# One idle product after the products with the inverse, in a chunked recurrence on one Trainium2 core

## The chip, the cores and the metric

The program runs on one core of one Trainium2 chip. The metric is the device time of one execution in microseconds (us); of several runs the median is taken. Engine names in the profile: PE is TensorE's products, PEld its weight loads, DVE is VectorE, ACT is ScalarE, POOL is GpSimd and SP is SyncE, which issues most DMAs. PEclk is the share of TensorE's clock that was granted: 0.50 is 1.2 GHz and 1.00 is 2.4 GHz.

## The reference

Three stages follow one another. The first is a recurrence over 768 time steps for 32 heads with a state of 40 by 40:

```python
for t in range(S):
    y[:, :, t] = einsum('bhd,bhde->bhe', r_t, state)
    Sa = einsum('bhde,bhe->bhd', state, a_t)
    state = state * w_t[:, :, None, :] - einsum('bhd,bhe->bhde', Sa, b_t) + einsum('bhd,bhe->bhde', v_t, k_t)
```

Its result is the input of a mixture of eight experts (top 2 of 8, 3072 tokens, width 320, inner width 1024), and that of a dense layer with inner width 2048 and a leaky rectifier, whose result is the output. Inputs and output are float32.

## The kernel before, in words

The recurrence is done in 12 chunks of 64 time steps. Inside a chunk the dependence of later steps on earlier ones is a triangular system. The kernel prepares, ahead of a chunk, decay factors by scans on VectorE (wq, lines 76 to 99), float16 stacks and their transposes by DMA (stack, tr, lines 101 to 107), score products (ks, lines 121 to 134), and the inverse of small diagonal blocks, which POOL builds row by row (t_step, line 148) and VectorE transposes into TT (t_fin, line 151).

The heads are handled in four groups of four pairs. Each group g has a PSUM bank of its own, bk[g] (128 partitions by 512 float32 columns). For each group a chunk takes four steps (two halves blk, two quarters h of 16 rows each). A step is:

- c_x (lines 163 to 174): products with the state (L170, recorded at the helper's line 167) and with what the chunk already has (also L167), into partitions 64 to 79 and 96 to 111 of bk[g]; ScalarE copies them to x (L174).
- c_u (lines 175 to 181): eight products of x with the inverse TT, 32 rows by 32 columns of the array each, in two bands (f = 0 and 1) into partitions 0 to 31 and 32 to 63 of the same bank (L179). A float32 product leaves two records in the trace, so one call of c_u leaves 16. Then ScalarE copies the two bands to VU (L181), which the next step of this group reads.

After the four steps c_s (lines 182 to 194) updates the group's state: products at L188, then VectorE (L190, L193) and POOL (L194). The output of the chunk (y_u, y_s, y_y, lines 196 to 222) follows, with products at L206, L214 and L219, and the router's logits of the next stage (L341 to L348).

The order of the work: run (line 226 on) gives each piece a key and traces the pieces in the order of the keys, so that the four groups are shifted against each other and the preparation runs about three chunks ahead. The TileContext (line 860) is built with schedule_with_timeline_sim=True: a planner then orders the instructions of every engine from their dependences. On the chip each engine runs its instructions in that fixed order. The constant s.idf (line 48) is the 128 by 128 float32 identity used for transposes.

The second stage has its products at L550 and L564, the third at L660 and L670; the change does not touch them.

Of the kernel before, what the change touches and what calls it, by code (L numbers as in the profile page):

```python
# [8 lines left out]
F16 = mybir.dt.float16  # L9
# [20 lines left out]
class Attn:  # L30
# [132 lines left out]
    def c_x(s,c,g,blk,h):  # L163
        nc=s.nc; K=s.K[c]; aT=s.aT[c%s.cfg['NA']]; VU=s.VU[c%2]; p0=64*(c%2); cs=slice(32*blk+16*h,32*blk+16*h+16); st=[True]*2
        px=s.bk[g]
        def mm(f,c0,n,l,r):
            q=64+32*f; nc.tensor.matmul(px[q:q+16,c0:c0+n],l,r,start=st[f],stop=True,skip_group_check=True); st[f]=False  # L167
        if c:
            for j in range(2):
                for f in range(2): i=4*g+2*j+f; mm(f,80*j,80,aT[:,i,cs],s.S[:,i,0:80])  # L170
        for z in range(4):
            for f in range(2): mm(f,40*z,40,K['g',f][:,4*g+z,cs],VU[:,f,4*g+z,:])
        x=s.x[g]
        nc.scalar.activation(x[p0:p0+48],px[64:112,0:160].rearrange("p (z d)->p z d",d=40),AF.Copy,scale=-0.125)  # L174
    def c_u(s,c,g,blk,h):
        nc=s.nc; TT=s.K[c]['TT']; VU=s.VU[c%2]; p0=64*(c%2); x=s.x[g]; n=32
        pu=s.bk[g][:,0:160].rearrange("p (a d)->p a d",a=4)
        for z in range(4):
            for f in range(2): nc.tensor.matmul(pu[32*f:32*f+n,z],TT[p0+32*f:p0+32*f+32,16*h:16*h+n,2*(4*g+z)+blk],x[p0+32*f:p0+32*f+32,z],start=h==0 and z==0,stop=True,skip_group_check=True)  # L179
        for f in range(2):  # L180
            q=64-64*f+32*blk; nc.scalar.activation(VU[q:q+n,f,4*g:4*g+4],pu[32*f:32*f+n],AF.Copy)  # L181
    def c_s(s,c,g):
# [681 lines left out]
```

## Time and profile before

| what | value |
|---|---|
| median of 3 runs | 1518.03 us (1511.66 to 1520.21) |
| profiled execution, its own time | 1532.47 us |
| its span (first to last instruction) | 1530.7 us |
| mean granted TensorE clock over the span | 0.87 |
| TensorE busy | 1215.9 us (79%) |
| VectorE busy | 892.4 us (58%) |
| ScalarE busy | 583.8 us (38%) |
| POOL busy | 481.8 us (31%) |

The profile is of one execution. Busy time is the union of the records of an engine; the ends of products are modelled, so a busy TensorE is not one at its peak. The chain of waits is followed back from the last instruction, at each step to what released it; its shares add up over the span or over the stretch that was asked for. Idle time of an engine that is not on that chain costs nothing by itself.

### The profile page before, as it was taken

How to read it: one execution, taken by the hardware profiler on the slowest of the kernel's cores; microseconds unless marked ns; L12 is line 12 of the kernel's file. 1: busy time of each engine (PE TensorE's matmuls, PEld its weight loads, DVE VectorE, ACT ScalarE, POOL GpSimd, SP SyncE). 2: the span in 40 equal slices, each digit the busy share in tenths (PEclk: the TensorE clock that was granted, in tenths of full speed). 3: DMA queues.
4: the chain of work that ended last, by engine and by line, in shares of the span. 5: the costliest groups of instructions: out<-in, count | busy, mean ns of one | idle time of the engine just before them, and what ended most of it. 6: DMA issues, size and time to landing. Idle time of an engine off the chain costs nothing.

```text
span 1530.7 us, 37727 instructions
## 1 busy us (share of the span) xinstructions
PE 1215.9 (79%) x15975; PEld 915.0 (60%) x15975; DVE 892.4 (58%) x2029; ACT 583.8 (38%) x1343; POOL 481.8 (31%) x559
## 2 busy tenths in 40 slices
PE   1358788878877879724879779779896799999998
PEld 0247677767766768624647557557575565555555
DVE  6897665664666487664654555679732764443221
ACT  1345345444545543431333223234321444334422
POOL 7464415224153252125222022030002526423422
PEclk9999776676888876757999889899998899999999
DMA  8679887768867755459745767375312522110000
GB/s 224 136 142 171 154 153 134 147 123 156 158 132 133 136 105 125 87 186 164 165 136 165 211 186 202 115 204 151 111 56 67 119 65 52 35 35 18 18 18 20
DMA packets 305937, 188.15 MB, mean 123 GB/s; under 512 B 260894, under 2 KB 276355, under 8 KB 304891
## 3 DMA queue, kind: packets, MB, share of 16 engines
q1 hardware_dynamic: 293103, 156.91, 46.6%
q0 software_dynamic: 10368, 16.84, 4.5%
q10 hardware_dynamic: 2288, 11.90, 2.4%
q8 instruction: 127, 2.08, 0.6%
q14 instruction: 51, 0.42, 0.1%
HBM read 105.24 MB, written 23.18 MB: 84 GB/s over the span
## 4 chain that ended last, share of the span: by engine, by line
PE 47%; DVE 20%; DMA 19%; POOL 5%; issue 4%; ACT 2%; SPq 2%; another core or an unknown queue 1%; ACTq 0%; DVEq 0%; POOLq 0%
PE ph L660 10%; PE po L670 10%; PE po L564 9%; PE ph L550 6%; DMA wf<-w 6%; PE bk L167 5%; DMA kbt<-stk 4%; PE bk L179 2%; DVE l L519 2%; DVE kb L99 2%; DMA w<-wi 2%; DMA N<-nd 1%; DVE Dt L82 1%; DVE S L193 1%; DMA nd<-ns 1%
## 5 line engine op out<-in xcount | busy, mean ns | idle before, releaser
L550 PE MATMUL ph<-xT,h 128*128 128x372 f16 (+2 forms) x680 | 151.2, 353 | 81.0 <-DVE gl L553 54.2
L552 ACT ACTIVATE gh<-ph 128x372 f16<-128x372 f32 (+2 forms) x136 | 68.1, 510 | 258.4 <-PE ph L550 245.9
L528 POOL DMA_INDIRECT xr<-xs,ix x56 | 81.4, 1453 | 254.9 <-DMA xT<-xr 234.2
L550 PEld LDWEIGHTS <-h 128*128 128x128 f16 x680 | 68.8, 102 | 126.5 <-issue 90.0
L664 POOL TENSOR_TENSOR gl<-hc,gh 128x512 f16<-128x512 f32 x80 | 91.9, 1157 | 146.7 <-ACT gh L663 146.5
L167 PE MATMUL bk<-S,aT 128*16 128x80 f32 x1408 | 113.5, 286 | 30.7 <-DVE S L193 20.9
L167 PE MATMUL bk<-VU,g 128*16 128x40 f32 x3072 | 135.1, 237 | 2.7 <-ACT VU L181 1.8
L181 ACT ACTIVATE VU<-bk 32x160 f32<-32x160 f32 x384 | 112.4, 293 | 62.3 <-PE bk L179 51.0
L564 PE MATMUL po<-h,gh 128*124 128x320 f16 x448 | 135.3, 304 | 1.0 <-ACT gh L552 0.6
L564 PE MATMUL po<-h,gl 128*124 128x320 f16 x448 | 134.5, 305 | 0.1
L564 PE MATMUL po<-l,gh 128*124 128x320 f16 x448 | 134.4, 303 | 0.0
L660 PE MATMUL ph<-xT,wih 128*128 128x512 f16 (+2 forms) x560 | 125.2, 354 | 7.8 <-DVE hc L662 4.5
L564 PEld LDWEIGHTS <-gh 128*124 128x124 f16 x896 | 122.7, 137 | 10.7 <-ACT gh L552 1.1
L662 DVE SCALAR_TENSOR_TENSOR hc<-ph,hc 128x512 f32<-128x512 f32 (+2 forms) x112 | 68.3, 612 | 98.2 <-ACT hc L661 97.2
L179 PE MATMUL bk<-x,TT 32*32 32x40 f32 x3072 | 122.8, 240 | 0.0
L670 PE MATMUL po<-woh,gh 128*128 128x320 f16 x384 | 114.1, 301 | 4.5 <-ACT gh L663 4.0
L167 PEld LDWEIGHTS bk<-VU,g 128*16 128x16 f32 x3072 | 111.1, 121 | 10.2 <-issue 4.2
L670 PE MATMUL po<-wol,gh 128*128 128x320 f16 x384 | 113.8, 301 | 0.0
L638 POOL DMA_INDIRECT yy<-yd,slot x48 | 48.7, 1014 | 204.0 <-DMA yd<-y 157.2
L179 PEld LDWEIGHTS bk<-x,TT 32*32 32x32 f32 x3072 | 103.4, 149 | 13.4 <-issue 3.8
L670 PE MATMUL po<-woh,gl 128*128 128x320 f16 x384 | 109.4, 301 | 0.0
L663 ACT ACTIVATE gh<-hc 128x512 f16<-128x512 f32 (+2 forms) x112 | 62.5, 566 | 119.2 <-PE po L670 66.4
(286 smaller groups left out, 2471.4 us busy)
## 6 DMA issues: line engine op xcount, KB each, us to landing
wf<-w SPq DMA_DIRECT2D x24, 512.0 KB
w<-wi SPq DMA_DIRECT2D x16, 768.0 KB
wf<-w SPq DMA_DIRECT2D x32, 320.0 KB
w<-wo SPq DMA_DIRECT2D x16, 640.0 KB
kb<-kb SPq DMA_DIRECT2D x24, 320.0 KB
yd<-y ACTq DMA_DIRECT2D x7, 1085.0 KB
w<-wz SPq DMA_DIRECT2D x24, 208.8 KB
aa<-aa SPq DMA_DIRECT2D x12, 320.0 KB
```

Of the source, the lines that this page charges most:

```text
L167: q=64+32*f; nc.tensor.matmul(px[q:q+16,c0:c0+n],l,r,start=st[f],stop=True,skip_group_check=True); st[f]=False
L179: for f in range(2): nc.tensor.matmul(pu[32*f:32*f+n,z],TT[p0+32*f:p0+32*f+32,16*h:16*h+n,2*(4*g+z)+blk],x[p0+32*f:p0+32*f+32,z],start=h== ...
L181: q=64-64*f+32*blk; nc.scalar.activation(VU[q:q+n,f,4*g:4*g+4],pu[32*f:32*f+n],AF.Copy)
L528: c=e*NJ+j; nc.gpsimd.indirect_dma_start(out=xr[0:PT,j],out_offset=None,in_=s.xs,in_offset=bass.IndirectOffsetOnAxis(ap=s.ix[0:PT,c:c+1],a ...
L550: for n,(t,k,i) in enumerate(ps): nc.tensor.matmul(ph[:,0:N],w(t,k,f),xT[:,j0:j1,i,0:PT],start=n==0,stop=n==7)
L552: nc.scalar.activation(o,ph[:,0:N],AF.Relu)
L564: nc.tensor.matmul(po[0:PT,0:DM],a[:,f,c],b[:,DM*f:DM*f+DM],start=n==0,stop=n==23); n+=1
L660: for n,(t,k,i) in enumerate(ps): nc.tensor.matmul(ph[:,0:N],w(t,k,f),xT[:,b0:b1,i,:],start=n==0,stop=n==7)
L662: nc.vector.scalar_tensor_tensor(c,ph[:,0:N],0.01,c,ALU.mult,ALU.max)
L663: nc.scalar.activation(gh[:,f,0:N],c,AF.Copy)
L664: (nc.vector if g<2 else nc.gpsimd).tensor_tensor(gl[:,f,0:N],c,gh[:,f,0:N],ALU.subtract)
L670: nc.tensor.matmul(po[:,0:DM],a[:,f,128*(b-b0):128*(b-b0)+128],bb[:,f,:],start=n==0,stop=n==47); n+=1
```

## The change

A new helper, warm, issues one matmul: the stationary operand is 64 columns, the moving operand 256 columns read twice (512 in all), both taken from the identity read as float16. It writes partitions 64 to 127 of the group's whole bank and starts a new accumulation there. Nobody reads the result: the next c_x or c_s of the group overwrites it. c_u calls it once, after its products and before the two copies to VU.

```diff
+    def warm(s,t):
+        w=s.idf.bitcast(F16); m=bass.AP(tensor=w.tensor,offset=w.offset,ap=[w.ap[0],[0,2],[1,256]])
+        s.nc.tensor.matmul(t[64:128,0:512],w[:,0:64],m,start=True,stop=True,skip_group_check=True)
     def c_u(s,c,g,blk,h):
         nc=s.nc; TT=s.K[c]['TT']; VU=s.VU[c%2]; p0=64*(c%2); x=s.x[g]; n=32
         pu=s.bk[g][:,0:160].rearrange("p (a d)->p a d",a=4)
         for z in range(4):
             for f in range(2): nc.tensor.matmul(pu[32*f:32*f+n,z],TT[p0+32*f:p0+32*f+32,16*h:16*h+n,2*(4*g+z)+blk],x[p0+32*f:p0+32*f+32,z],start=h==0 and z==0,stop=True,skip_group_check=True)
+        s.warm(s.bk[g])
         for f in range(2):
             q=64-64*f+32*blk; nc.scalar.activation(VU[q:q+n,f,4*g:4*g+4],pu[32*f:32*f+n],AF.Copy)
```

## Rows read from the trace of the kernel before

**Rows 1.** The page: busy tenths and granted clock in 40 equal slices.
```profile
PE   1358788878877879724879779779896799999998
...
PEclk9999776676888876757999889899998899999999
```

**Rows 2.** Busy time by stretch; columns as in the first line, one stretch a row.
```profile
core 0: us, PE busy (x) PEld busy (x) DVE busy (x) ACT busy (x) POOL busy (x), PEclk, DMA share, GB/s
...
97.00:650.00 553.00, 451.44 (x11083) 393.30 (x11083) 369.56 (x912) 269.40 (x766) 199.10 (x309) 0.77 0.72 137
```

**Rows 3.** The chain that ended last, whole program: by engine, and by line.
```profile
PE 47%; DVE 20%; DMA 19%; POOL 5%; issue 4%; ACT 2%; SPq 2%; another core or an unknown queue 1%; ACTq 0%; DVEq 0%; POOLq 0%
...
by line: PE ph L660 9.7%; PE po L670 9.5%; PE po L564 8.8%; PE ph L550 6.3%; DMA wf<-w 5.6%; PE bk L167 4.8%; issue 4.2%; DMA kbt<-stk 4.1%; PE bk L179 2.1%; DVE l L519 1.8%; DVE kb L99 1.6%; DMA w<-wi 1.5%; DMA N<-nd 1.4%; DVE Dt L82 1.4%;
```

**Rows 4.** The chain from 97 to 650 us, by line.
```profile
by line: PE bk L167 13.1%; DMA kbt<-stk 10.6%; issue 6.3%; PE bk L179 5.9%; DVE S L193 3.7%; DMA nd<-ns 3.3%; DMA N<-nd 3.3%; DVE kb L99 3.1%; DVE Dt L82 2.5%; DMA ut<-us 2.4%; DMA kb<-kb 2.4%; DVE stk L106 2.1%; POOL T L148 1.9%; DMA kb<-x
```

**Rows 5.** The page's groups: busy us, mean ns of one, idle before them.
```profile
L179 PE MATMUL bk<-x,TT 32*32 32x40 f32 x3072 | 122.8, 240 | 0.0
```

**Rows 6.** Waits, 97 to 650 us: us in total, times, longest.
```profile
ACT x L174 <- PE bk L167: 123.5, 116, 6.5
...
ACT VU L181 <- PE bk L179: 51.0, 61, 5.3
```

**Rows 7.** The chain in order of time, 261 to 296 us: start, length, what.
```profile
254.37 6.87 DMA kbt<-stk
261.29 0.48 PE sc L129 x8
...
265.54 0.67 PE bk L179 x14
...
275.30 0.68 PE bk L179 x16
...
282.18 0.52 PE pt L95 x4
282.72 0.48 DVE kb L99
```

**Rows 8.** Busy time by stretch inside that period; columns as in rows 2.
```profile
258.00:261.00 3.00, 1.59 (x65) 1.28 (x60) 0.33 (x2) 0.60 (x2) 2.53 (x7) 0.99 0.73 134
...
264.00:266.00 2.00, 2.00 (x51) 1.58 (x49) 1.68 (x5) 1.19 (x5) 0.31 (x2) 0.50 1.05 75
...
278.00:280.00 2.00, 2.00 (x30) 1.50 (x27) 0.00 (x0) 0.93 (x4) 0.00 (x0) 0.50 0.22 82
...
282.00:285.00 3.00, 3.00 (x111) 2.68 (x108) 2.40 (x6) 1.69 (x4) 1.49 (x2) 1.00 0.12 29
```

**Rows 9.** The chain in order of time, third stage, clock 1.00.
```profile
1265.08 1.73 PE ph L660 x8
```

**Rows 10.** TensorE in order of time, second stage, clock 0.50: start, length, instruction.
```profile
909.18 2.23 PE L550 MATMUL ph<-xT,h 128*128 128x496 f16 x5 [8.25 <-DVE gl L553]
911.20 1.45 PE L550 MATMUL ph<-xT,l 128*128 128x496 f16 x3
```

**Rows 11.** TensorE in order of time, recurrence, clock 0.50.
```profile
275.23 0.75 PE L179 MATMUL bk<-x,TT 32*32 32x40 f32 x16
275.90 0.71 PE L167 MATMUL bk<-S,aT 128*16 128x80 f32 x6
276.55 1.28 PE L179 MATMUL bk<-x,TT 32*32 32x40 f32 x32
277.76 0.31 PE L167 MATMUL bk<-S,aT 128*16 128x80 f32 x1
```

**Rows 12.** What TensorE's products waited for, 97 to 650 us.
```profile
PE bk L167 <- DVE S L193: 20.9, 9, 4.4
PE sc L129 <- DMA kbt<-stk: 20.4, 11, 3.6
...
PE bk L167 <- ACT VU L181: 11.4, 11, 2.7
```

## The prediction

> **What bounds the kernel now.** I read the page's slices first, to find the stage in which the changed function runs. TensorE is at seven tenths or more from the fourth slice on, and its granted clock is full at the start and for most of the second half; in slices 5 to 17 between them it reads six to eight tenths [rows 1]. The table by stretch makes this exact: the recurrence runs from 97 to 650 us, TensorE (PE) is busy 451.44 of 553 us, the mean granted clock is 0.77, and the 16 DMA engines are 72% busy [rows 2]. As the clock has two levels, 1.2 GHz (0.50) and 2.4 GHz (1.00), a mean of 0.77 is about half of the time at each.
>
> Next the chain of waits. Over the whole program PE holds 47% of it, but most of that lies behind the recurrence [rows 3]. Cut to the recurrence, the chain is mixed: the products that make x (L167) 13.1%, the products with the inverse (L179) 5.9%, and besides them DMA transposes, VectorE lines and the block inverse on POOL [rows 4]. So TensorE ends the stage for part of the time only, and no engine for all of it. The groups give the sizes: L179, the line behind which the change puts its product, is 122.8 us of busy time in 3072 records, and PE sat idle 0.0 us before it [rows 5]. Twice a step it is ScalarE that waits for TensorE: the x copy 123.5 us for L167, the VU copy 51.0 us for L179 [rows 6].
>
> Last I went through one period. The chain runs from the DMA transpose that ends at 261.24 through 30 pieces of PE alone, 21 us, to 282.70, and then goes over to VectorE [rows 7]. In the middle of these 21 us, in each of the eight stretches from 264 to 280, PE is busy 2.00 of 2.00 us and the clock is 0.50 all the same; from 282 to 285 it is 1.00 [rows 8]. Of the pieces in it, L179 has a gap of ten us, from the 14 records at 265.54 to the 16 at 275.30 [rows 7].
>
> **The change, part by part.** Nothing is removed. Each of the 192 calls of c_u (12 chunks, 4 groups, 4 steps; 3072 records are 192 times 16) gets one weight load and one product. No DMA is added or moved, and no queue of SP or POOL is passed. The product reads a constant and writes partitions 64 to 127 of the group's bank. The x copy has read them before c_u can begin, since c_u reads x, so the product adds no wait of its own; the VU copies read partitions 0 to 63. What it does is to stand in TensorE's queue: behind it are the next products of another group, mostly c_x, c_u or c_s, and behind those ScalarE and VectorE.
>
> *Length.* The trace has such a product in another stage. A 128x512 f16 product takes 1.73/8 = 0.216 us at clock 1.00 [rows 9]. At 0.50, five products of 496 columns take 911.20-909.18 = 2.02 us, 0.404 each, so 0.42 us for 512 columns [rows 10]. The bounds are 0.22 and 0.42.
>
> *Change of shape.* The inverse products use 32 rows by 32 columns of the array; the x products use 128 rows. One c_u of 16 records is followed by an x product after 275.90-275.23 = 0.67 us, two of 32 records after 277.76-276.55 = 1.21 us; so 16 records cost 0.54 us, and 0.13 us is left for the change of shape [rows 11]. The idle product (128 by 64) fits neither neighbour, so I count one more such change for each, 0.13 us; the lower bound is nothing, the upper 0.26 where the next one is again a c_u. Total per product: 0.35 us at 1.00, 0.55 us at 0.50. The Trainium skill, TensorEngine Tiling (Array Packing), section Key Properties, says that a change of tiling mode, unlike a change of tile, drains TensorE; by that rule every idle product pays it going in or out, and it speaks against the change. The 0.13 us of the row agrees. Without any drain the sum below would be about 7 us lower.
>
> *How many are on the path.* L179 has 2.1% of the whole chain, 0.021 x 1530.7 = 32 us, out of 122.8 us busy: 26%, or 50 of 192 calls [rows 3, 5]. These cost 50 x 0.35 = 17.5 to 50 x 0.55 = 27.5 us. The 21 us of PE alone lie at 0.50, so I take a value towards the upper end: 24 us.
>
> *The other 142* are in stretches where something else is late: 142 x 0.35 to 0.55 is 50 to 78 us of new TensorE work, covered by the 553-451 = 102 us in which PE is idle now [rows 2]. What hides it is PE's waits for the state update (20.9 us), the transposed kbt (20.4 us) and the VU copy (11.4 us) [rows 12]. Where such a cover is shorter than the products ahead of it, the remainder shows. Bounds: none, or all that exceeds the cover; with some 64 us against 102 us spread unevenly I take 10 us.
>
> *What the clock gives back.* If the products lift the clock, the chain's PE work shrinks. The two lines have 4.8% + 2.1% of the chain, 105 us [rows 3]; were all of it at 0.50 now and at 1.00 after, 52 us would be saved. The other bound is nothing. I take 9 us, near nothing, for three reasons in the rows. First, PE was busy without a break from 264 to 280 us and stayed at 1.2 GHz [rows 8], so a fuller TensorE alone doesn't raise it; the product there puts off other products and fills no pause. Second, it stands behind c_u and not in the waits: the clock read 0.99 from 258 to 261 us, when PE was busy 1.59 of 3 us, and was 0.50 afterwards [rows 8], and a product of 0.2 us issued ahead of a wait leaves most of that wait empty. Third, there are ten us without c_u in that very stretch [rows 7]. The Trainium skill, TensorE: Matmul & The Clock Gate, section Why this matters for your kernels, advises to keep TensorE busy to have the full clock; by that advice the saving would be near the 52 us. Rows 8 disagree for this kind of product.
>
> **Sum:** 24 + 10 - 9 = +25 us. Against the profiled execution, 1532.47 us (span 1530.70 and 1.77 around it), that gives 1557. The profiled execution lies 14.4 us above the median of the three runs, 1518.03; with the same difference the median becomes **1543 us**.
>
> **Rivals.**
> *A, the clock rises (faster).* The idle product is 512 columns of 128 rows where c_u fills 32 rows, and it comes 192 times, so it could hold TensorE at 2.4 GHz through most of the stage. For: about half of the stage is at 0.50, and the chain's longest PE stretch with it [rows 2, 7, 8]. Against: the three reasons above. Time: of the 52 us that L167 and L179 can save, 40; the products at full clock cost 50 x 0.35 = 17.5 us: 1518 - 22 = 1496. It decides if the granted clock from 97 to 650 us goes above about 0.9.
>
> *B, no change.* The planner, which orders the instructions from the program's dependences, puts the products where PE would wait anyway, or what they cost and what the clock gives back are equal: 1518. This is also the case of a change that does nothing. For: PE idles 102 us of the stage [rows 2]. Against: it is idle 0.0 us before L179 [rows 5], and the product follows at once.
>
> *C, the step's own loop becomes longer.* If the VU copies are held until the idle product is over (the bank guarded as a whole), each exposed step waits 0.35 to 0.55 us more. ScalarE waited for L179 in 61 places already [rows 6]; nothing in the regions (0 to 63 against 64 to 127) requires it. With half of the 192 steps exposed, 96 x 0.45 = 43 us on top: 1518 + 25 + 43 = 1586.
>
> **How the numbers follow.** Forecast 0.55, A 0.22, B 0.15, C 0.08. About 0.5% (7.6 us) is what a measurement of this kernel can tell from no change; faster is A (0.22), same is B (0.15), slower is the forecast with C (0.63). The forecast's own range comes from its bounds, 17.5 + 0 - 9 to 27.5 + 20 - 0: 1527 to 1565. The stated range reaches to B and to the weaker half of A on one side, 1503, and towards C on the other, 1572; some 0.1 is left out at each end.
>
> **What would show it.** In the new profile: 192 products of 512 columns, of 0.22 to 0.42 us each; the recurrence about 25 us longer, TensorE's busy time in it up by 50 us or more, its granted clock between 0.75 and 0.85, the stages behind it unchanged; in the period shown, still long PE stretches at 0.50. I am wrong about the clock if the mean is above 0.9; about the cover if PE's idle time stays near 100 us while the stage gets longer; about C's cause if the VU copies begin only after the idle product's end.

## The result, and the profile after

The changed kernel takes 1526.07 us (median of 20 runs, 1513.46 to 1542.87) where the kernel before takes 1518.11 (20 runs, 1505.41 to 1524.99). The ratio of the mean times is 1.0061, 95% interval 1.0035 to 1.0088: slower by 0.0061 x 1518 = 9 us, with 5 to 13 inside the interval. Two of the 20 runs of the change, 1540.33 and 1542.87 us, were in a slower state and are left out of the ratio. The sign was forecast, the size was not: 25 us were forecast.

The two traced executions would tell the opposite (span 1520.3 us after, 1530.7 before), since the one of before lies 14 us above its median and the one after 4 us below. So I read the recurrence by itself. First the time at which the first and the last VU copy start, in the kernel before, in a second trace of it, in the change and in a second trace of the change (line numbers have moved by four):

```profile
L181 ACT ACTIVATE VU<-bk x384: 291/294/296, 100.6 to 649.0; 32x160 f32<-32x160 f32 x192
```

```profile
L181 ACT ACTIVATE VU<-bk x384: 291/294/296, 102.1 to 644.3; 32x160 f32<-32x160 f32 x192
```

```profile
L185 ACT ACTIVATE VU<-bk x384: 292/294/297, 103.3 to 650.7; 32x160 f32<-32x160 f32 x192
```

```profile
L185 ACT ACTIVATE VU<-bk x384: 291/294/298, 103.2 to 651.2; 32x160 f32<-32x160 f32 x192
```

The last copy starts at 649.0 and 644.3 us before, at 650.7 and 651.2 after. The page's slices and the table by stretch of the change answer to [rows 1, 2]:

```profile
PE   1358899988998999934879779797896899999998
...
PEclk9998788888889997856999999899998899999999
```

```profile
97.00:650.00 553.00, 500.97 (x11242) 399.67 (x11242) 366.17 (x916) 267.94 (x764) 201.92 (x311) 0.85 0.71 137
```

TensorE's busy time has gone up by 501 - 451 = 50 us, as forecast, and the granted clock from 0.77 to 0.85. In this window of 553 us TensorE is idle 52 us where it was 102. The chain of the same stretch shows what this means, against [rows 4]; the second line is that of the second trace of the change:

```profile
by line: PE bk L167 13.8%; PE bk L182 10.4%; DMA kbt<-stk 9.5%; PE bk L177 6.0%; issue 4.8%; DMA N<-nd 3.1%; DMA nd<-ns 2.9%; DMA ut<-us 2.3%; DVE kb L99 2.3%; POOL tmp L148 2.2%; POOL T L148 2.1%; PE bk L192 2.1%; DVE S L197 2.0%; PE yy L2
```

```profile
by line: PE bk L167 11.7%; DMA kbt<-stk 9.7%; PE bk L182 8.6%; issue 5.3%; PE bk L177 4.7%; DMA N<-nd 3.8%; DMA ut<-us 3.3%; POOL tmp L148 3.2%; POOL T L148 2.9%; DMA nd<-ns 2.5%; DMA kb<-kb 2.0%; DVE S L197 1.7%; DVE kb L99 1.7%; DMA kb<-x
```

L177 is the idle product: 6.0% of 553, 33 us of the chain, and 4.7%, 26 us, in the second trace. Counted along the chain from 97 to 650 us, 85 of the 192 idle products stand in it, and 69 in the second trace. The products with the inverse (L182 now) have risen from 5.9% to 10.4% and 8.6%: more of the stage waits for TensorE than before. One period in order of time, the counterpart of [rows 7]:

```profile
254.49 6.32 DMA kbt<-stk
260.85 0.61 PE sc L129 x8
...
262.60 0.56 PE bk L177
263.17 0.69 PE yy L223 x32
...
274.44 0.33 PE bk L177
274.77 0.53 PE bk L167 x16
...
279.32 0.52 PE pt L95 x4
```

The stretch of PE alone begins at 260.85 instead of 261.29 and ends at 279.84 instead of 282.70, though six idle products stand in it; each takes 0.56 us of the chain at 1.2 GHz and 0.33 at 2.4. Its clock, against [rows 8]:

```profile
268.00:270.00 2.00, 2.00 (x23) 1.31 (x24) 1.23 (x3) 0.59 (x2) 0.36 (x2) 0.50 1.03 208
270.00:272.00 2.00, 2.00 (x56) 1.74 (x52) 1.94 (x4) 0.30 (x1) 0.00 (x0) 0.72 1.25 183
272.00:274.00 2.00, 2.00 (x54) 1.91 (x54) 1.89 (x11) 0.41 (x2) 0.62 (x1) 1.00 1.31 90
```

It rises at about 271 us, after three idle products; before, it read 0.50 in every stretch up to 280. One period shows what happened in it and no more; that the clock follows the product is read from the mean over the recurrence. Last, the waits of ScalarE, against [rows 6], and two places in order of time:

```profile
ACT x L174 <- PE bk L167: 88.0, 112, 4.0
ACT VU L185 <- PE bk L177: 85.2, 118, 3.3
```

```profile
267.35 0.47 PE L182 MATMUL bk<-x,TT 32*32 32x40 f32 x6
...
267.75 0.95 PE L95 MATMUL pt<-idf,Dt 104*128 104x104 f32 x4
...
268.64 0.64 PE L177 MATMUL bk<-idf 128*64 128x512 f16 x1
...
269.31 0.60 ACT L185 ACTIVATE VU<-bk 32x160 f32<-32x160 f32 x2 [1.94 <-PE bk L177]
```

The VU copies wait for the idle product (L177) and not for the products whose result they read: here those are done before 268, the planner has put transposes between them and the product, and the copies start at the product's end. In both traces of the change none of the 192 pairs starts before its product's end, although the copies read partitions 0 to 63 and the product writes 64 to 127. So the program guards them against each other whatever the partitions; whether it goes by the whole bank or by the columns, which overlap in every version, no run separates. The wait of the VU copies rose from 51.0 to 85.2 us. That of the x copies fell from 123.5 to 88.0, so that the two together stay where they were, 174.5 and 173.2 us.

### The profile page after: what moved, and what is told of

The parts are those of the page before. It is cut to its first block, busy times and chain, and to the rows that moved or that the text cites. A ratio compares the mean times of both kernels' runs of the same rounds, so it can differ in the third digit from the quotient of the medians.

```text
span 1520.3 us, 38111 instructions
## 1 busy us (share of the span) xinstructions
PE 1260.7 (83%) x16167; PEld 917.8 (60%) x16167; DVE 887.5 (58%) x2029; ACT 583.3 (38%) x1343; POOL 484.9 (32%) x559
## 4 chain that ended last, share of the span: by engine, by line
PE 50%; DMA 20%; DVE 18%; POOL 4%; issue 3%; ACT 2%; SPq 2%; ACTq 0%; DVEq 0%; POOLq 0%
PE ph L664 9%; PE po L674 9%; PE po L568 8%; DMA wf<-w 7%; PE ph L554 6%; PE bk L167 5%; PE bk L182 4%; DMA kbt<-stk 4%; PE bk L177 2%; DVE l L523 2%; DMA N<-nd 2%; DVE wam L513 1%; DVE kb L99 1%; DVE Et L88 1%; DMA nd<-ns 1%
## 5 line engine op out<-in xcount | busy, mean ns | idle before, releaser
L182 PE MATMUL bk<-x,TT 32*32 32x40 f32 x3072 | 149.3, 234 | 4.1 <-issue 2.3
L182 PEld LDWEIGHTS bk<-x,TT 32*32 32x32 f32 x3072 | 115.5, 145 | 43.7 <-issue 20.7
L167 PE MATMUL bk<-VU,g 128*16 128x40 f32 x3072 | 114.3, 223 | 0.0
L167 PE MATMUL bk<-S,aT 128*16 128x80 f32 x1408 | 99.8, 266 | 9.8 <-ACT VU L185 4.7
L513 DVE TENSOR_REDUCE wam<-wf 128x1 f32<-128x1024 f32 (+1 forms) x35 | 46.3, 1325 | 98.2 <-DMA wf<-w 97.9
```

## The experiments

Every ratio is to the kernel before on the same chip, in five rounds; chips differ by some 10 us (before: 1516 to 1526), so ratios are compared. The granted clock is that of 97 to 650 us. In the traces of the change, e2 and e3 all other instructions come in one and the same order; e1, e5, e6 and e11 share a second one; each other run with an idle product has its own.

**Once more before, once more after.**

> The kernel before, once more, for a second trace of it and to see what two equal programs differ by. Every theory: 0.997 to 1.003, the granted clock in the recurrence 0.76 to 0.79. Theory 'order' (a part of what the products do is that the planner puts the other instructions in another order) wants the recurrence to end near 650 us here, against 635 us with the 32 by 32 product of 16 columns; if it ends near 640 us, most of that difference was chance in one trace.

> The changed kernel on the same chip as the others: 1.003 to 1.009 of before, clock 0.84 to 0.86 in the recurrence. If chips differ in what the clock gives back, it can lie outside, between 0.998 and 1.012.

Measured: 1.0002 (0.9971 to 1.0034) and 1.0076 (1.0040 to 1.0113). The stretch from 97 to 650 us, of before and of the change:

```profile
97.00:650.00 553.00, 455.04 (x11110) 396.08 (x11112) 376.53 (x923) 270.03 (x767) 204.17 (x312) 0.76 0.71 137
```

```profile
97.00:650.00 553.00, 500.82 (x11241) 401.55 (x11241) 365.62 (x916) 266.98 (x764) 202.21 (x310) 0.85 0.71 137
```

The clocks and TensorE's busy times repeat. The last VU copy of the second trace of before, 644.3 us, lies between the 650 and the 640 that the expectation named. The change costs 9 to 12 us.

**Length and clock, at the change's own order.** e3 keeps the product and cuts it to 16 columns; e2 keeps its 512 columns and fills 32 of the 128 rows.

```diff
-        w=s.idf.bitcast(F16); m=bass.AP(tensor=w.tensor,offset=w.offset,ap=[w.ap[0],[0,2],[1,256]])
-        s.nc.tensor.matmul(t[64:128,0:512],w[:,0:64],m,start=True,stop=True,skip_group_check=True)
+# e3
+        w=s.idf.bitcast(F16); m=bass.AP(tensor=w.tensor,offset=w.offset,ap=[w.ap[0],[1,16]])
+        s.nc.tensor.matmul(t[64:128,0:16],w[:,0:64],m,start=True,stop=True,skip_group_check=True)
+# e2
+        w=s.idf.bitcast(F16)[0:32]; m=bass.AP(tensor=w.tensor,offset=w.offset,ap=[w.ap[0],[0,2],[1,256]])
+        s.nc.tensor.matmul(t[64:128,0:512],w[:,0:64],m,start=True,stop=True,skip_group_check=True)
```

> The idle product keeps its shape (128 by 64), place and count and has 16 columns in place of 512. What is left is the change of shape and the wait of the VU copies behind it. 'Clock gives back': clock 0.76 to 0.78, time 1.004 to 1.010 of before, for 50 products on the path at some 0.13 to 0.3 us. 'Covered': 0.998 to 1.003.

> As the run with 32 by 32, but 32 rows by 64 columns, a shape that none of its neighbours has. 'Clock gives back': clock 0.76 to 0.81, time 1.015 to 1.03 of before; above the 32 by 32 run by the price of the change of shape, some 5 us. 'Covered': 1.003 to 1.009, as the change.

Measured: e3 1.0037 (1.0011 to 1.0062), e2 1.0168 (1.0142 to 1.0194). Of e2 the stretch and the chain of the stretch:

```profile
97.00:650.00 553.00, 516.00 (x10809) 406.49 (x10810) 351.94 (x854) 258.94 (x738) 200.53 (x312) 0.76 0.68 134
```

```profile
by line: PE bk L167 21.4%; PE bk L182 15.2%; PE bk L177 9.4%; DMA kbt<-stk 7.0%; issue 4.2%; PE bk L192 3.5%; PE sc L129 2.8%; PE ys L210 2.7%; PE yy L223 2.6%; DMA ut<-us 2.2%; DVE kb L99 2.0%; PE yy L351 1.6%; PE pt L91 1.4%; DMA kb<-kb 1
```

and of e3 the stretch; then the VU copies of e2 and of e3:

```profile
97.00:650.00 553.00, 494.39 (x11160) 429.10 (x11159) 362.12 (x899) 266.77 (x761) 201.84 (x309) 0.76 0.71 135
```

```profile
L185 ACT ACTIVATE VU<-bk x384: 291/294/298, 103.8 to 675.7; 32x160 f32<-32x160 f32 x192
```

```profile
L185 ACT ACTIVATE VU<-bk x384: 291/294/297, 102.8 to 659.3; 32x160 f32<-32x160 f32 x192
```

Three runs with one order now stand in a row: a product of hardly any length costs 0.37%, 6 us; the full length at the same clock of 0.76 costs 1.68% x 1526 = 26 us, so length is 20 us; and the product of 128 rows, which has the same length and a clock of 0.85, costs 9 us (12 on the other chip), so the clock gives back 14 to 16 us. By their intervals each of these differences can be off by 6 or 7 us; e2 and e3 ran on one chip, the change on two others. The last VU copy gives the same order: 659.3 us in e3, 675.7 in e2, 650.7 and 651.2 in the change, so 16 us for the length and 25 back.

That e2's array shape is another than the change's could be a rival to the clock. The chain speaks against it: at the same clock one idle product takes as long in e2 as in the change, 0.56 and 0.33 us.

```profile
262.54 0.56 PE bk L177
...
269.29 0.33 PE bk L177
```

For e2 this is "clock gives back" and not "covered", which wanted 1.003 to 1.009; e3, 1.0037, lies between the two theories. Above the 32 by 32 run by some 5 us, as expected too, e2 is not: it is 40 us above it. And a share of the chain is no price: 118 idle products with 52 us (9.4% of 553) stand in e2's chain, and the kernel is 26 us slower.

**The held copies.** e4 issues the product behind the two copies instead of ahead of them.

```diff
-        s.warm(s.bk[g])
         for f in range(2):
             q=64-64*f+32*blk; nc.scalar.activation(VU[q:q+n,f,4*g:4*g+4],pu[32*f:32*f+n],AF.Copy)
+        s.warm(s.bk[g])
```

> The idle product is issued behind the two VU copies, not ahead of them, so that the copies no longer wait for it and it waits for them. If the held copies are a good part of the cost (rival C), the clock stays at 0.83 to 0.87 and the time falls to 0.992 to 1.001 of before. If they cost nothing, it is 1.003 to 1.009 as the change. If TensorE's own wait for the copies is worse, over 1.012.

Measured: 1.0077 (1.0048 to 1.0105), with the clock at 0.85 again.

```profile
97.00:650.00 553.00, 490.82 (x11136) 384.63 (x11138) 363.40 (x898) 266.77 (x758) 201.29 (x309) 0.85 0.71 135
```

Without held copies it is no faster. There the product waits for the copies in place of the other way round, and the order is another, so this doesn't prove that holding them is free; it shows that nothing is won by turning the wait about.

```profile
PE bk L177 <- ACT VU L184: 11.4, 10, 2.5
```

**More of it, and another order for the same shape.** e8 calls warm twice in a row; e15 uses 48 stationary columns, w[:,0:48] into t[64:112], in place of 64.

> The change's product twice in each call, 384 products in all. The second has the shape of the first, so it adds length and work for the clock but no change of shape. If length is cheap and the clock pays for it: clock 0.88 or more in the recurrence, 1.000 to 1.008 of before. If length costs what 34 us for 192 products suggest less what the clock still gives: 1.012 to 1.030.

> The change's product, 128 rows and 512 columns, with 48 stationary columns in place of 64: the array shape (128 by 64) and the work over time are nearly the same, but the planner puts the other instructions in another order. 'Order' moves it by up to 10 thousandths: 0.997 to 1.015, clock 0.83 to 0.87. If order plays no part for this shape: 1.005 to 1.009, as the change.

Measured: e8 1.0247 (1.0209 to 1.0285) at a clock of 0.90; e15 1.0049 (1.0015 to 1.0083) at 0.85. The stretch of e8:

```profile
97.00:650.00 553.00, 501.32 (x10804) 368.16 (x10805) 350.87 (x823) 255.20 (x725) 196.86 (x305) 0.90 0.67 131
```

With a second product the clock goes from 0.85 to 0.90 and the time up by 1.7 to 1.9%, some 27 us: the clock doesn't pay for it, though e8's own order is in this too. e15, the change's shape in another order, comes out as the change does within the noise.

**Shape.** e1, e5, e6 and e11 use 32 stationary columns into t[64:96] and share one order. e1 has 32 rows and 512 columns, e5 32 rows and 16 columns (the shape of the products with the inverse), e6 128 rows and 512 columns, e11 128 rows and 16 columns (the shape of the products for x).

```diff
+# e5 (e1: 512 columns; e6: all rows of s.idf, 512 columns; e11: all rows, 16 columns)
+        w=s.idf.bitcast(F16)[0:32]; m=bass.AP(tensor=w.tensor,offset=w.offset,ap=[w.ap[0],[1,16]])
+        s.nc.tensor.matmul(t[64:96,0:16],w[:,0:32],m,start=True,stop=True,skip_group_check=True)
```

> The idle product keeps its 512 columns, its place and its count, and uses 32 rows by 32 columns of the array, the shape of the products with the inverse, in place of 128 by 64. Theory 'clock gives back' (the 192 products cost 25 us or more, and the rise of the granted clock from 0.77 to 0.85 in the recurrence pays for most of it): the clock stays at 0.76 to 0.79 and the time is 1.015 to 1.03 of before (1541 to 1564 us). Theory 'covered' (most products lie in time that TensorE had idle, and the clock matters little): 1.003 to 1.009, the same as the change, whatever the clock does.

> The 32 by 32 idle product with 16 columns in place of 512: same place, count, shape and wait of the VU copies, hardly any work. Theory 'clock' (the 32 by 32 product was faster than before because its 512 columns raise the granted clock, 0.77 to 0.80 in the recurrence): clock 0.76 to 0.78 and 0.998 to 1.004 of before. Theory 'order' (the planner's other order of the instructions made it faster, the product itself does nothing): 0.988 to 0.994 as with 512 columns.

> The idle product as in the change, 128 rows and 512 columns, but 32 stationary columns: the shape of the products for x, which often come next. Theory 'shape' (the change's cost is mainly the extra change of shape before and after the product): one change less where an x product follows, 0.994 to 1.003 of before with the clock at 0.82 to 0.86. Theory 'length' (its cost is the 512 columns): 1.004 to 1.010, as the change.

> The idle product with 128 rows, 32 stationary columns and 16 columns: the planner's order is the same, instruction by instruction, as with the 32 by 32 product of 16 columns (0.989), and only the array shape differs. Theory 'shape': 0.997 to 1.005 of before, 8 to 16 thousandths above that run. Theory 'order' alone (shape costs next to nothing, and the change's order of instructions is the slower one): 0.988 to 0.992.

Measured: e1 0.9907 (0.9879 to 0.9934), e5 0.9889 (0.9855 to 0.9923), e6 0.9962 (0.9934 to 0.9990), e11 0.9974 (0.9941 to 1.0007). The stretches of e1, e5, e6 and e11 in this order:

```profile
97.00:650.00 553.00, 452.48 (x11423) 386.43 (x11423) 376.75 (x936) 270.07 (x769) 211.04 (x316) 0.80 0.73 140
```

```profile
97.00:650.00 553.00, 453.33 (x11415) 393.65 (x11414) 374.04 (x929) 268.07 (x766) 208.45 (x313) 0.79 0.74 139
```

```profile
97.00:650.00 553.00, 497.33 (x11423) 392.36 (x11423) 375.59 (x935) 269.76 (x769) 209.91 (x316) 0.86 0.72 140
```

```profile
97.00:650.00 553.00, 495.40 (x11374) 427.68 (x11375) 373.64 (x928) 269.18 (x767) 208.75 (x313) 0.77 0.72 140
```

My expectation for e1 was off by 1 to 4% on either theory: in the shape of its neighbours the full product is nearly free. TensorE's busy time shows where the two shapes differ. It stays at 452 to 453 us in the shape of the products with the inverse, whether the product has 16 columns or 512, and is 495 to 497 us in the other. From e5 to e11, 16 columns each and the same order, the price of the shape, with the clock that goes with it (0.79 and 0.77), is 0.9974 - 0.9889 = 0.0085, 13 us, or 0.07 us for each of the 192 products; by the two intervals it can be 6 to 20 us. The two kept traces do not show it in the recurrence: the last VU copy starts at 637.5 us in e11 and at 635.4 in e5 (both lines follow below). e5's trace is of the slowest of its six runs. From e11 to e6, length and clock (0.77 to 0.86) together are -0.0012, nothing: they cancel here too. Both runs came out where "shape" put them.

But e5 also shows something that no theory had: a product of hardly any work makes the kernel 1.1% faster than before (where "order" put it, and "clock" did not), with the last VU copy at 635.4 us. Of e5 and e11:

```profile
L185 ACT ACTIVATE VU<-bk x384: 291/294/297, 102.1 to 635.4; 32x160 f32<-32x160 f32 x192
```

```profile
L185 ACT ACTIVATE VU<-bk x384: 291/294/297, 101.5 to 637.5; 32x160 f32<-32x160 f32 x192
```

**Order or held copies.** e12 is e5 with 16 stationary columns, in a third order; e13 issues e5's product ahead of the products with the inverse, so that no copy is held; e14 issues it behind the copies.

> The 32 by 32 idle product of 16 columns with 16 stationary columns in place of 32: the same array shape, hardly less work, but the planner puts the other instructions in a third order. Theory 'order' with chance (each order has its own time): anywhere from 0.985 to 1.005 of before. If the gain of the 32 by 32 run comes from the wait of the VU copies or from the product itself, 0.986 to 0.992 again.

> The 32 by 32 product of 16 columns, issued ahead of the products with the inverse in place of behind them: the VU copies wait for c_u's own products alone, as before the change. Theory 'order' (the planner's new order gave the 0.6 to 1.1% of the two runs with such a small product): another order, and a gain or loss by chance, 0.985 to 1.005. Theory 'held copies' (the copies that wait for the product make the gain, by bringing TensorE's products closer together): 0.998 to 1.003.

> The 32 by 32 product of 16 columns, issued behind the two VU copies: no copy is held, the product waits for the copies. 'Order': 0.985 to 1.005, by chance. 'Held copies': 0.999 to 1.006, no gain left.

Measured: e12 0.9936 (0.9901 to 0.9971), e13 1.0020 (0.9990 to 1.0050), e14 1.0098 (1.0064 to 1.0131). The two orders with held copies gain, the two without don't, and e14 lies above both theories. As each of the four has an order of its own, the gain can't be put down to the copies. Nor is it shown to be the order's: the four, between 0.989 and 1.010 with next to no added work, differ in order and in place at once, and say that the two together can be worth 1% either way. Where order alone differs, between e5 and e12 and between the change and e15, the ratios are 0.005 and 0.001 to 0.003 apart, which the intervals do not tell from nothing.

**Another place, and two small products.** e16 puts a product of 128 rows, 32 stationary columns and 512 columns ahead of each step's products for x; e7 issues two of 32 by 32 and 512 columns on the row bands that the chunk doesn't use.

> A product of 128 rows, 32 stationary columns and 512 columns, issued just ahead of each step's products for x and in their array shape: no further change of shape, no held VU copy, and it stands where TensorE waits for the copies. If shape and place were the cost and the clock the gain: clock 0.84 to 0.88 and 0.980 to 0.994 of before. If the length of the product counts wherever it stands: 0.996 to 1.012.

> Two idle products of 32 by 32 and 512 columns in each call, on the two row bands that this chunk's products with the inverse don't use, beside each other. If such tiles run beside the products with the inverse and the array's filled share is what lifts the clock: clock 0.81 to 0.86 in the recurrence, time 0.980 to 0.990 of before. If their length counts: 1.00 to 1.02.

Measured: e16 1.0032 (1.0002 to 1.0063) at a clock of 0.84; e7 1.0094 (1.0059 to 1.0129) at 0.79. e16 came out where "length counts" put it; that shape and place were all of the cost has fallen, as far as its own order lets one say. e7's time, too, lies where "their length counts" put it, but TensorE's busy time has not grown:

```profile
97.00:650.00 553.00, 444.81 (x11468) 381.78 (x11468) 370.22 (x907) 267.84 (x764) 200.46 (x309) 0.79 0.71 137
```

Its clock did not rise to the 0.81 to 0.86 of the other theory, and it is slower than e1, which has one such product; its order is its own, so the cause stays open.

Faster than the kernel before with their whole interval are e5, e1, e12 and e6, at 0.989, 0.991, 0.994 and 0.996. For e5 and e12, whose product does hardly any work, this is not the merit of TensorE's added work.

## Why the prediction was right or wrong

**The price of one product: right. Their number on the path: too low.** I priced one product at 0.35 us at 2.4 GHz and 0.55 us at 1.2 GHz; its pieces in the chain are 0.33 and 0.56 us. I took 50 products with 24 us on the path; the chain has 85 with 33 us in one trace of the change and 69 with 0.047 x 553 = 26 us (4.7% for L177) in the other. That 26 comes near 24 is in part luck: more products are on the path, and more of them at the full clock, than I took. The 50 came from the chain before, and the change moved the chain towards TensorE.

**The cost without the clock: too high.** The sum had 24 + 10 = 34 us before anything is given back. e2, which has the change's place, length, order and held copies, at a clock of 0.76, costs 26 us (22 to 30). The first step that failed is therefore the sum of path and remainder, 34 us, sized as if each piece that stands in the chain, and 10 us beside them, made the kernel longer by its own length: in e2 the chain holds 52 us of idle products and the kernel is 26 us longer, so about half of what stands in the chain seems to have taken the place of another wait. How the 26 us divide between the 24 and the 10 is not shown. e2's order and its held copies are in them as well, and e5 and e14 show that order and place together move the time by 1% either way, so I can't say that the cover as such was better than I thought.

**What the clock gives back: too low.** The second step is this term. I took 9 us, "near nothing, for three reasons in the rows"; measured are 14 to 16 us, the change against e2, with 9 at the edge of what the intervals allow, and 25 us by the last VU copy. The first reason holds as a sentence, "a fuller TensorE alone doesn't raise it": e2 is fuller and stays at 0.76. What failed is what I drew from it for this product. With the float16 product of 128 rows the clock of the recurrence is 0.85, with 32 rows and the same length 0.76. That the clock rose at 271 us in the period shown, where it had stayed at 1.2 GHz to 280, is not enough for that: in e2, too, it is full for a part of this period.

```profile
268.00:270.00 2.00, 2.00 (x65) 1.54 (x64) 0.00 (x0) 1.27 (x5) 1.69 (x5) 1.00 0.03 8
```

The second reason, that the product fills no pause, and the third, ten us without c_u, went with the order: TensorE's idle time fell from 102 to 52 us, and the longest gap between idle products in that stretch is 5.7 us (268.71 to 274.44). The Trainium skill, TensorE: Matmul & The Clock Gate, section Why this matters for your kernels, advises to keep TensorE busy. e2 speaks against that as the whole of the rule: TensorE is busiest there, 516.00 of 553 us, and its clock, 0.76, no higher than before. The change agrees with it.

Both errors point the same way, 34 to 26 and 9 to 14 or 16, and so 25 became 9 to 12.

**The change of shape: right in kind.** I counted one more change for each product, 0.13 us, and some 7 us on the path. e11 against e5 gives 13 us for 192 products that leave the shape of the products with the inverse. That agrees with the Trainium skill, TensorEngine Tiling (Array Packing), section Key Properties, by which a change of tiling mode drains TensorE: the same 16 columns cost TensorE 42 us of busy time more in the other shape (495.40 against 453.33). The run doesn't part a drain from the loss of the overlap that e1 shows (last section). That it is also the term to attack, I did not see.

**The waits: wrong.** I wrote that the product "adds no wait of its own" because its partitions are others. None of the 192 pairs of copies starts before its end. This is rival C's mechanism; its price, 43 us on top, did not come: the whole change costs 9 to 12 us, and e4, without held copies, is no faster.

**Rival A** had the direction of the clock (0.85, not the 0.9 at which it would decide), and e8 shows that 0.90 can be had but not for its price. **Rival B** had the two sides nearly equal, and was closer to the time than the forecast was.

**What the prediction lacked** is a term for the planner. I treated the order of the other instructions as given; a new instruction gives a new order, and new waits with it, and the range should have had some 1% each way for the two together. One reading was loose, without consequence: TensorE is not at seven tenths or more in all slices from the fourth on; three of them, all behind the recurrence, read 2, 4 and 6.

## What to carry to other kernels

In a shape that its neighbours don't have, an idle product that was to hold TensorE's clock was paid for by its length, 20 us here, and by the change of array shape; the one of 128 rows brought the clock up and the one of 32 rows did not. Measure clock and price separately, with two such products of the same length and in the same order, before believing either. Give such a product the shape of its neighbours, where its length cost next to nothing (e1), and look in the built program at who waits for its bank. When a planner orders the instructions, compare variants that have the same order, and treat a difference of 1% between different orders as unexplained until one such pair shows it.

## What the runs showed that I had not expected

A product of 32 by 32 with 512 columns behind the products with the inverse adds no busy time to TensorE (452.48 us with it, 451.44 and 455.04 before) and 0.0018 to the ratio against 16 columns, less than the noise, though 192 such products at 0.22 to 0.42 us would be 42 to 81 us one after the other. The trace of e1 shows such a product beside products with the inverse and not ahead of them:

```profile
271.19 0.60 PE L177 MATMUL bk<-idf 32*32 32x512 f16 x1
271.19 0.61 PE L182 MATMUL bk<-x,TT 32*32 32x40 f32 x18
```

Two of them on other row bands add no busy time either (e7, 444.81 us), and yet that kernel is 0.9% slower; why, was not tried. And the gain of e5 and e12 over the kernel before, 0.6 to 1.1%, is left open between the order and the held copies.
